# The fourth group's output in seven products, x added to the products of the last three groups, the last substitution spread into the fifth period, two scalings moved to VectorE

## The chip, the cores and the metric

The kernel runs on one core of a Trainium2 chip. The metric is the device time of one execution in microseconds; lower is better. All arithmetic is float32.

## The reference

Two blocks follow each other. The first is a delta-rule recurrence over 768 tokens for each of 4 batches and 8 heads of 48 dimensions; the second is a feed-forward layer with a maximum over three hidden projections, for 3072 tokens of width 384 and a hidden width of 768.

```python
k_n = k / (np.linalg.norm(k, axis=-1, keepdims=True) + 1e-06)
for t in range(S):
    kt, vt, bt = (k_n[:, :, t], v[:, :, t], beta[:, :, t, None])
    y[:, :, t] = np.einsum('bhd,bhde->bhe', q[:, :, t], state)
    v_old = np.einsum('bhde,bhd->bhe', state, kt)
    state = state + bt[:, :, :, None] * np.einsum('bhd,bhe->bhde', kt, vt - v_old)
...
x = attn_out.transpose(0, 2, 1, 3).reshape(B * S, H * D)
h = np.maximum(np.maximum(x @ w1, x @ w2), x @ w3)
out = h @ w_out
```

## The kernel before

**Chunks and groups.** The recurrence is solved in 12 chunks of 64 tokens. A chunk needs a triangular inverse, which VectorE finds by substitution: `solve(m)` does it for the two chunks of group `m` at once, in 31 steps of a pair of operations, a product into `tmp` (L563) and a subtraction (L567). The generator `solving` is stepped by `some(solving, n)`. When it ends, `solve` writes the result to DRAM (`y_d`, L588) and reads it back in another layout into `ut` (L597), both on SyncE's queue. The products `z` and `j` (`join_z`, `join_u`) complete the inverse; `new` (p_u) gives the chunk's new values, from the scaled values `v_t` less what the state already holds (`old_k`: p_k on TensorE, then L754 on VectorE); `step` (p_s) adds to the state `st` (L800); `to_y` (p_y, L814) gives the chunk's output y.

**From y to x.** `y_blocks` writes y to DRAM (`y_x`), `read_y` reads it back into `qall`, both on SyncE's queue, and `turn_y` (L872) transposes it on VectorE into `xt`, the x of the feed-forward layer.

**Periods.** Two chunks make a group of 512 tokens, and there are six groups, `m` = 0 to 5, here the first to the sixth. `ffn(m)` is a generator that runs the feed-forward layer of group `m`: one period. After each of its units it yields, and the loop at the end of the kernel puts in pieces of the recurrence of group `m + 1` by the tables `LINKS` and `LAST_LINKS`. In them, a letter is a piece and a digit its chunk or block: k, q, z, j, u, s and y are the products above; d the transposes `turn_t1`; x is `y_blocks`, w `read_y`, X `turn_y`; V loads values and P or p scales them; K loads keys; L and N load blocks; t and g turn them and form the key products. The entry 17 of `LINKS` puts X1 after unit 17. The order of instructions on each engine is the order in which the code issues them; nothing reorders it. So where VectorE waits, all that the code issued later for VectorE waits too.

**Hidden layer.** In the second to the fifth period a period has six hidden tiles of 128 columns for two differences of weights, 12 units, each of three matmuls 512 wide (p_h, L1170); ScalarE takes the first of a tile (L1180), VectorE the maximum (L1184). The sixth does it in products of quarters (`crossed_hidden`), whose weights `cross_hidden` makes in the fifth period (L1072). It makes sums of quarters of x as well (L1094 to L1097).

**Output.** For the first four groups `ffn` multiplies four token tiles with `wo_sb` (six matmuls 384 wide) and, from the second group on, adds x times `w_sb[0]` (three more), both L1209. For the fifth and sixth group `outputs` does it in seven products of halves (L971): the halves of h, three matrices each, are added and subtracted on VectorE (`op`, L1000) before the products, the results after them, and the two banks p and q are used in turn. The x part stands outside the seven products there, as plain products `x_times` of three slices for each quarter of the result. `cross_weights` makes the combinations of `wo_sb` that the seven products need, on VectorE, in the fifth period, after units 8 and 9 (L925 to L944).

**Banks.** `ps_ffn` has two PSUM banks until the sixth period, and p_h, p and q share them. A product into a bank starts when the last reader of the bank is done.

**Scaling.** `scale` (L298) multiplies the values of chunk `c` with their norms, on GpSimd for all chunks.

Of the kernel before, what the change touches and what calls it, by code (L numbers as in the profile page):

```python
# [9 lines left out]
FP32 = mybir.dt.float32  # L10
# [4 lines left out]
ALU = mybir.AluOpType  # L15

C = 64
# [6 lines left out]
def kernel(  # L24
# [31 lines left out]
    nc = tc.nc  # L56
# [5 lines left out]
    KT = DM // 128  # L62
    FT = DFF // 128
    NP = H // 2
    UNITS = NCH * 2
    GROUPS = UNITS // 4
# [22 lines left out]
    def ps_ffn(shape, name):  # L89

        one = len(pools) > 1
        return pools[-1].tile(shape, FP32, name=name, tag="ffn", bufs=8 if one else 2)
# [202 lines left out]
            nrms[2 * m + cc] = t[:, 16:32].rearrange("p (g h) -> p g h", g=2)  # L295

    def scale(c, nrm):
        nc.gpsimd.tensor_tensor(  # L298
            out=vts[c], in0=vts[c],
            in1=nrm[:, :, :, None].to_broadcast([128, 2, H, D]), op=ALU.mult,  # L300
        )
# [16 lines left out]
    def square(name):  # L318
        return work.tile([128, H, C], FP32, name=name, tag="square", bufs=17)
# [594 lines left out]
    HALF = DM // 2  # L914
# [3 lines left out]
    def cross_weights(part):  # L918

        left, right = slice(0, HALF), slice(HALF, DM)  # L920
        top, bottom = wo_sb[:, 0:PAIRS], wo_sb[:, PAIRS:FT]
        spare = w_sb[0][:, :, DM : 2 * DM]
        minus = nc.vector.tensor_tensor
        if part == 0:
            minus(  # L925
                out=spare[:, :, right], in0=bottom[:, :, right], in1=top[:, :, right],
                op=ALU.subtract,
            )
            minus(
                out=top[:, :, right], in0=top[:, :, right], in1=top[:, :, left],  # L930
                op=ALU.subtract,
            )
            return
        minus(
            out=spare[:, :, left], in0=bottom[:, :, right], in1=top[:, :, right],
            op=ALU.subtract,
        )
        fourth = []
        for n in range(2):
            t = work.tile([128, DM], FP32, name="mant", bufs=2)  # L940
            for i in range(2 - n):
                fourth.append(t[:, HALF * i : HALF * (i + 1)])
        for j in range(PAIRS):
            minus(  # L944
                out=fourth[j], in0=wo_sb[:, PAIRS + j, left], in1=spare[:, j, left],
                op=ALU.subtract,
            )
        crossed.update(
            b11=[top[:, j, left] for j in range(PAIRS)],
            b21=[bottom[:, j, left] for j in range(PAIRS)],  # L950
            b22=[bottom[:, j, right] for j in range(PAIRS)],
            t1=[top[:, j, right] for j in range(PAIRS)],
            t2=[spare[:, j, left] for j in range(PAIRS)],
            t3=[spare[:, j, right] for j in range(PAIRS)],
            t4=fourth,
        )

    def outputs(m, hs):


        xt, w = xts[m], crossed
        a11, a21, a12, a22 = (
            [hs[j + d][:, lo : lo + 256] for j in range(PAIRS)]
            for d, lo in ((0, 0), (0, 256), (PAIRS, 0), (PAIRS, 256))
        )
        p, q = (ps_ffn([128, 2, HALF], "p_o") for _ in range(2))

        def times(to, a, b, start=True, stop=True):
            for g in range(2):
                for j in range(PAIRS):  # L970
                    nc.tensor.matmul(  # L971
                        to[:, g], a[j][:, 128 * g : 128 * (g + 1)], b[j],
                        start=(start and g == j == 0),
                        stop=(stop and g == 1 and j == PAIRS - 1),
                    )

        def x_times(to, lo, right, start=False, stop=True):
            times(
                to,
                [xt[:, t, lo : lo + 256] for t in range(KT)],  # L980
                [w_sb[0][:, t, HALF * right : HALF * (right + 1)] for t in range(KT)],
                start, stop,
            )

        def held(name, dtype_bufs):
            return work.tile([128, 2, HALF], FP32, name=name, bufs=dtype_bufs)

        def store(o, cc, right, queues=one_queue):
            cols = slice(HALF * right, HALF * (right + 1))
            s0 = (2 * m + cc) * C  # L990
            for n in range(2):
                queues[n].dma_start(
                    out=out.rearrange("(b s) d -> b s d", s=S)[
                        2 * n : 2 * n + 2, s0 : s0 + C, cols
                    ].rearrange("g c x -> c g x"),
                    in_=o[rows(n)],
                )

        def op(to, a, b, how):
            nc.vector.tensor_tensor(out=to, in0=a, in1=b, op=how)  # L1000

        plus, minus = ALU.add, ALU.subtract
        times(p, a11, w["b11"])
        m1 = held("m1", 1)
        nc.scalar.copy(m1, p)
        yield
        sums = [square("s").rearrange("p h c -> p (h c)") for _ in range(PAIRS)]
        s14, s32 = ([s[:, lo : lo + 256] for s in sums] for lo in (0, 256))
        for j in range(PAIRS):
            op(s32[j], a11[j], a21[j], minus)  # L1010
        for j in range(PAIRS):
            op(s14[j], a21[j], a22[j], plus)
        times(q, a12, w["b21"], True, False)
        yield
        x_times(q, 0, 0)
        c11 = held("o_sb", 2)
        op(c11, m1, q, plus)
        store(c11, 0, 0)
        yield
        times(p, s32, w["t3"])  # L1020
        m7 = held("o_sb", 2)
        nc.scalar.copy(m7, p)
        yield
        times(q, s14, w["t1"])
        m5 = held("up", 2)
        nc.scalar.copy(m5, q)
        for j in range(PAIRS):
            op(s32[j], s14[j], a11[j], minus)
        yield
        times(p, s32, w["t2"])  # L1030
        m6 = held("up", 2)
        nc.scalar.copy(m6, p)
        for j in range(PAIRS):
            op(s14[j], a12[j], s32[j], minus)
        yield
        x_times(q, 0, 1, True, False)
        op(m6, m6, m1, plus)
        op(m7, m7, m6, plus)
        yield
        times(p, a22, w["t4"], True, False)  # L1040
        op(m6, m6, m5, plus)
        op(m5, m5, m7, plus)
        yield
        x_times(p, 256, 0)
        op(m7, m7, p, plus)
        store(m7, 1, 0)
        yield
        times(q, s14, w["b22"], False)
        op(m6, m6, q, plus)
        store(m6, 0, 1)  # L1050
        yield
        x_times(p, 256, 1, True)
        op(m5, m5, p, plus)
        store(m5, 1, 1, both_queues)
        yield

    thirds = {}

    def cross_hidden(i):

# [17 lines left out]
    def crossed_hidden(m, hs):  # L1078
# [16 lines left out]
        vec(out=s1, in0=a21, in1=a22, op=ALU.add)  # L1095
        vec(out=s2, in0=s1, in1=a11, op=ALU.subtract)
        vec(out=s4, in0=a12, in1=s2, op=ALU.subtract)  # L1097
        for j in range(FT):
            hs[j] = square("h").rearrange("p h c -> p (h c)")
        for unit in range(2 * PAIRS):  # L1100
# [58 lines left out]
    def ffn(m):  # L1159
# [35 lines left out]
            early = FT  # L1195
        for f in range(early, FT):
            yield from hidden(f, 0, TOK)
        if m >= GROUPS - 2:
            yield from outputs(m, hs)
            return  # L1200
        for i in range(4):
# [21 lines left out]
    def some(gen, n):  # L1223
        for _ in range(n):
            if next(gen, gen) is gen:
                break
# [102 lines left out]
        5: "g2 g3 p1", 6: "u0 N0", 7: "V1 N1", 8: "s0 y0 N2", 9: "x0", 10: "k1 q1",  # L1329
        11: "u1 w0", 13: "y1 x1 s1", 14: "X0 w1", 16: "P0", 17: "X1 K0 K1 K2 K3",  # L1330
    }
    LAST_LINKS = {**LINKS, 17: "", 19: "X1"}
    EARLY_LINKS = {
        9: "k0 q0", 10: "t0", 11: "t1", 12: "g0", 13: "t2", 14: "g1", 15: "t3",
        16: "g2", 17: "g3", 18: "d0 d1 z0 z1", 19: "j0", 20: "j1 u0", 21: "s0",
# [22 lines left out]
    def links(m, names):  # L1358
        for name in names.split():
            f, i = name[0], int(name[1])  # L1360
            if f in RECURS and m < GROUPS:
                RECURS[f](2 * m + i)
            elif f in MADE and m + 1 < GROUPS:
                MADE[f](2 * (m + 1) + i)
            elif f in UNIT and m + 1 < GROUPS:
                UNIT[f](4 * (m + 1) + i)
            elif f == "N" and m + 2 < GROUPS:
                load_blocks(4 * (m + 2) + i)
# [67 lines left out]
    MADE.update(V=lambda c: load_v(c, nc.gpsimd))  # L1436
    for m in range(1, GROUPS):
        for i, _ in enumerate(ffn(m)):
            if i == 0:
                some(solving, 3)  # L1440
            if m == 1 and i in (2, 5, 8):
                both_layers(i // 3)
            if m == GROUPS - 2 and i in (4, 5):
                cross_hidden(i - 3)
            if m == GROUPS - 2 and i in (8, 9):
                cross_weights(i - 8)
            if m + 2 < GROUPS:
                if i == 6:
                    blocks(m + 2)
                if i == 8:  # L1450
                    solving = solve(m + 2)
            links(m + 1, (LAST_LINKS if m == GROUPS - 2 else LINKS).get(i, ""))
            if i > 7:
                some(solving, 3 if i > 8 else 1)
    by_hand.close()
# [28 lines left out]
```

## Time and profile before

| | |
|---|---|
| Median of 3 runs | 511.67 us (509.7 to 511.67) |
| Profiled execution | 512.05 us, its span 510.2 us |
| TensorE busy | 489.5 us, 96% of the span |
| VectorE busy | 349.8 us, 69% |
| ScalarE, GpSimd busy | 168.8 us, 192.7 us |
| Fourth period | 316.4 to 389.2 us |
| Fifth period | 389.2 to 455.7 us |
| Sixth period | 455.7 to 510.2 us |
| TensorE, output of the fourth group | 363.9 to 389.2 us |
| TensorE, output of the fifth and the sixth | 432.1 to 455.1 us, 484.3 to 505.9 us |

Times are from one execution taken by the hardware profiler. PE is TensorE, DVE VectorE, ACT ScalarE, POOL GpSimd, SP SyncE; SPq is SyncE's queue, which issues DMAs. A row of an order in time gives the start, the duration, the engine, the line, the operation, what it writes and reads, and how often; in brackets stands how long the engine was idle before it and what ended that. A float32 matmul has two records.

### The profile page before, as it was taken

How to read it: one execution, taken by the hardware profiler on the slowest of the kernel's cores; microseconds unless marked ns; L12 is line 12 of the kernel's file. 1: busy time of each engine (PE TensorE's matmuls, PEld its weight loads, DVE VectorE, ACT ScalarE, POOL GpSimd, SP SyncE). 2: the span in 40 equal slices, each digit the busy share in tenths (PEclk: the TensorE clock that was granted, in tenths of full speed). 3: DMA queues.
4: the chain of work that ended last, by engine and by line, in shares of the span. 5: the costliest groups of instructions: out<-in, count | busy, mean ns of one | idle time of the engine just before them, and what ended most of it. 6: DMA issues, size and time to landing. Idle time of an engine off the chain costs nothing.

```text
span 510.2 us, 18525 instructions
## 1 busy us (share of the span) xinstructions
PE 489.5 (96%) x8016; PEld 333.6 (65%) x8016; DVE 349.8 (69%) x801; ACT 168.8 (33%) x320; POOL 192.7 (38%) x317
## 2 busy tenths in 40 slices
PE   7678989999999999999999999999999999999996
PEld 6567768855566555565555565555565556988896
DVE  5887789977997341799562988554988446458752
ACT  5585655785422142210153200252101321112310
POOL 7434462793491935780485690601230000000000
PEclk9855889999999999999999999999999999999999
DMA  8937869674045934454585354834334302230001
GB/s 111 202 53 213 189 148 168 172 182 144 3 125 132 192 64 99 123 124 109 120 156 128 106 136 96 167 52 90 91 80 97 67 1 62 50 78 2 0 17 46
DMA packets 106304, 53.49 MB, mean 105 GB/s; under 512 B 89712, under 2 KB 99984, under 8 KB 106224
## 3 DMA queue, kind: packets, MB, share of 16 engines
q1 hardware_dynamic: 94352, 31.35, 30.2%
q0 software_dynamic: 9472, 20.37, 16.0%
q8 instruction: 63, 1.03, 0.9%
q10 hardware_dynamic: 2400, 0.59, 0.6%
q14 instruction: 17, 0.14, 0.1%
HBM read 39.17 MB, written 13.11 MB: 102 GB/s over the span
## 4 chain that ended last, share of the span: by engine, by line
PE 77%; DVE 7%; DMA 6%; ACT 4%; SPq 3%; issue 2%; POOL 0%; DVEq 0%; ACTq 0%; POOLq 0%
PE p_h L1170 28%; PE p_o L1209 17%; PE p_o L971 8%; PE p_e L1113 3%; PE p_c L1113 3%; PE p_u L770 2%; PE p_g L417 2%; PE p_m L905 2%; DMA qall<-in_q_dram 2%; PE p_s L793 2%; DMA kmore<-in_k_dram 2%; PE p_y L812 2%; SPq L131 2%; PE p_k L742 2%; PE p_j L725 2%
## 5 line engine op out<-in xcount | busy, mean ns | idle before, releaser
L1170 PE MATMUL p_h<-xt,w_sb 128*128 128x512 f32 (+1 forms) x450 | 188.9, 562 | 0.7 <-ACT xt L838 0.6
L1170 PEld LDWEIGHTS p_h<-xt,w_sb 128*128 128x128 f32 x450 | 83.2, 195 | 69.0 <-issue 61.8
L1209 PE MATMUL p_o<-wo_sb,h 128*128 128x384 f32 x192 | 65.3, 490 | 0.0
L1184 DVE TENSOR_TENSOR h<-h,p_h 128x512 f32<-128x512 f32 (+1 forms) x42 | 25.5, 607 | 54.1 <-PE p_h L1170 53.4
L563 DVE TENSOR_TENSOR tmp<-x_bl,y_bl 128x31 f32<-128x31 f32 (+20 forms) x139 | 51.2, 368 | 4.1
L567 DVE TENSOR_TENSOR y_bl<-y_bl,tmp 128x31 f32<-128x31 f32 (+20 forms) x139 | 48.5, 349 | 4.8
L1209 PEld LDWEIGHTS p_o<-wo_sb,h 128*128 128x128 f32 x192 | 35.7, 190 | 23.2
L375 POOL DMA_DIRECT2D turned<-in_q_dram x72 | 39.3, 553 | 5.4 <-POOL turned L370 3.1
L1215 ACT COPY o_sb<-p_o 128x384 f32<-128x384 f32 x16 | 7.7, 479 | 85.8 <-PE p_o L1209 79.7
L1180 ACT ACTIVATE h<-p_h 128x512 f32<-128x512 f32 x24 | 14.3, 597 | 62.9 <-PE p_h L1170 59.9
L265 POOL TENSOR_TENSOR w_sb<-mant,up 128x384 int32<-128x384 int32 x18 | 18.8, 1044 | 41.2 <-DVE mant L261 39.1
L417 PEld LDWEIGHTS p_g<-kqt 48*64 48x64 f32 x1216 | 24.1, 138 | 9.3 <-issue 6.2
L417 PE MATMUL p_g<-kqt 48*64 48x64 f32 (+1 forms) x1216 | 27.4, 238 | 1.0 <-ACT kqt L346 0.8
L800 DVE TENSOR_TENSOR st<-st,p_s 48x768 f32<-48x768 f32 (+1 forms) x18 | 17.1, 949 | 15.4 <-PE p_s L793 15.2
L131 POOL DMA_DIRECT2D kpad<-in_k_dram x32 | 21.9, 692 | 14.0 <-issue 12.6
L1209 PE MATMUL p_o<-w_sb,xt 128*128 128x384 f32 x72 | 25.2, 486 | 0.0
L401 DVE TENSOR_TENSOR pt<-p_g,mask 128x512 f32<-128x512 f32 x20 | 13.8, 689 | 16.1 <-PE p_g L417 15.8
L150 POOL DMA_DIRECT2D v_t<-in_v_dram x14 | 11.6, 831 | 34.7 <-PE p_u L770 34.7
L298 POOL TENSOR_TENSOR v_t<-v_t,nrm 128x768 f32<-128x768 f32 x12 | 17.9, 1495 | 9.0 <-DVE nrm L292 8.9
L370 POOL MEMSET turned<- 128x96 f32 x18 | 3.3, 192 | 46.9 <-DVE kqt L391 46.9
L770 PEld LDWEIGHTS p_u<-v_t,ut 64*64 64x64 f32 x768 | 13.5, 141 | 9.8 <-issue 8.6
L1209 PEld LDWEIGHTS p_o<-w_sb,xt 128*128 128x128 f32 x72 | 13.7, 190 | 9.5
(212 smaller groups left out, 835.4 us busy)
## 6 DMA issues: line engine op xcount, KB each, us to landing
out_dram<-o_sb SPq DMA_DIRECT2D x40, 96.0 KB
w_bits<-in_moe_w_dram SPq DMA_DIRECT2D x9, 384.0 KB
w_bits<-in_moe_w_dram POOLq DMA_DIRECT2D x9, 384.0 KB, 5.1
turned<-in_q_dram POOLq DMA_DIRECT2D x72, 48.0 KB, 2.9
kpad<-in_k_dram POOLq DMA_DIRECT2D x32, 96.0 KB, 5.5
y_x<-y SPq DMA_DIRECT2D x16, 192.0 KB
qall<-y_x SPq DMA_DIRECT2D x32, 96.0 KB
v_t<-in_v_dram POOLq DMA_DIRECT2D x14, 192.0 KB, 4.8
```

The costliest lines, as they stand in the source:

```text
L131: queues[bb].dma_start(out=dst[rows(bb ^ g), :, 0:D], in_=src[2 * bb + g, :, c * C : (c + 1) * C, :].rearrange("h p d -> p h d"),)
L265: nc.gpsimd.tensor_tensor(out=dst.bitcast(I32), in0=mant_v.bitcast(I32), in1=up_v, op=ALU.add)
L375: (queue, nc.gpsimd)[i].dma_start(out=t[p0 : p0 + 32, bb, at : at + NP * 2 * D].rearrange("p (j x) -> p j x", j=NP), in_=(k, q)[i][2 * bb ...
L417: nc.tensor.matmul(p_g[rows(bb ^ (g * i)), par, c0 : c0 + C * (1 + whole)], kq[:, 0], kq if whole else kq[:, i],)
L563: nc.vector.tensor_tensor(out=t_v, in0=row.to_broadcast(t_v.shape), in1=column.to_broadcast(t_v.shape), op=ALU.mult,)
L567: nc.vector.tensor_tensor(out=rest, in0=rest, in1=t_v, op=ALU.subtract)
L770: nc.tensor.matmul(p_v[rows(bb ^ g), g, i], ut[c % NU][rows(bb), g, h], rhs[rows(bb), g, h],)
L971: nc.tensor.matmul(to[:, g], a[j][:, 128 * g : 128 * (g + 1)], b[j], start=(start and g == j == 0), stop=(stop and g == 1 and j == PAIRS - 1),
L1113: nc.tensor.matmul(to, w[stays], moves, start=(n == 0), stop=(n == len(terms) - 1))
L1170: nc.tensor.matmul(p_h, w_sb[i][:, t, f * 128 : (f + 1) * 128], xt[:, t, lo : lo + w], start=(t == 0), stop=(t == KT - 1),)
L1184: nc.vector.tensor_tensor(out=h, in0=h, in1=p_h, op=ALU.max)
L1209: nc.tensor.matmul(p_o, stays, moves, start=(n == 0), stop=(n == len(terms) - 1))
```

## The change

The fourth group's output is done by `outputs` too. In `outputs`, two of the three slices of x join the halves of h: each of the four quarters gets one more matrix, so a product has 8 matmuls instead of 6, and `x_times` keeps one slice, 2 matmuls instead of 6. A group's output has 7 x 8 + 4 x 2 = 64 matmuls of 192 columns; before, the fifth and sixth had 7 x 6 + 4 x 6 = 66, and the fourth 36 of 384. `cross_weights` gets a third part, four subtractions on 128x192, for the weights of x; its three parts now run in the fourth period after units 5, 6 and 10. The sums of x are made with those of h in the fourth and fifth period, in four matrices instead of three; the sixth uses those that `crossed_hidden` makes anyway. In the fourth period the sums lie in `kmore`.

The fourth and fifth period get tables of their own. In the fourth (now of 23 units) the turns X0 and X1 go from units 14 and 17 to 15 and 18, the scaling P0 from 16 to 21. The substitution of the last group was ended within the fourth period and the first three steps of the fifth; now 20 steps are taken in the fourth and 17 in units 0 to 5 of the fifth. The products that need its result go later there: z from unit 3 to 7, j to 8, the first u from 6 to 9, s and y from 8 to 10, k and q of the second chunk from 10 to 11, the second u to 12. `scale` runs on VectorE for chunks 10 and 11.

```diff
     def scale(c, nrm):
-        nc.gpsimd.tensor_tensor(
+        (nc.vector if c > 9 else nc.gpsimd).tensor_tensor(
...
+        if part == 2:
+            x11, x12, x21, x22 = (w_sb[0][:, t, lr] for t in range(2) for lr in (left, right))
+            free = work.tile([128, NP, 2, 2, C], FP32, name="kqt", bufs=6)
...
+            for to, a, b in ((x3, x22, x12), (x1, x12, x11), (x2, x22, x1), (x4, x21, x2)):
+                minus(out=to, in0=a, in1=b, op=ALU.subtract)
+            for name, x in dict(
+                b11=x11, b21=x21, b22=x22, t1=x1, t2=x2, t3=x3, t4=x4
+            ).items():
+                crossed[name].append(x)
+            return
...
+        for a, t, lo in ((a11, 0, 0), (a21, 0, 256), (a12, 1, 0), (a22, 1, 256)):
+            a.append(xt[:, t, lo : lo + 256])
...
         def x_times(to, lo, right, start=False, stop=True):
             times(
                 to,
-                [xt[:, t, lo : lo + 256] for t in range(KT)],
-                [w_sb[0][:, t, HALF * right : HALF * (right + 1)] for t in range(KT)],
+                [xt[:, KT - 1, lo : lo + 256]],
+                [w_sb[0][:, KT - 1, HALF * right : HALF * (right + 1)]],
                 start, stop,
             )
...
-        sums = [square("s").rearrange("p h c -> p (h c)") for _ in range(PAIRS)]
+        n = len(x_sums.get(m, ())) == 0
+        if m == GROUPS - 3:
+            sums = [
+                t.rearrange("p a h d -> p (a h d)")[:, lo : lo + 512]
+                for t in kmore
+                for lo in (0, 512)
+            ]
+        else:
+            sums = [
+                square("s").rearrange("p h c -> p (h c)") for _ in range(PAIRS + n)
+            ]
         s14, s32 = ([s[:, lo : lo + 256] for s in sums] for lo in (0, 256))
-        for j in range(PAIRS):
-            op(s32[j], a11[j], a21[j], minus)
-        for j in range(PAIRS):
-            op(s14[j], a21[j], a22[j], plus)
+        s1, s2, s3, s4 = s14, s32, s32, s14
+        if not n:
+            s1, s2, s3, s4 = (s + [x] for s, x in zip((s1, s2, s3, s4), x_sums[m]))
+        for j in range(len(sums)):
+            op(s3[j], a11[j], a21[j], minus)
+        for j in range(len(sums)):
+            op(s1[j], a21[j], a22[j], plus)
...
-        if m >= GROUPS - 2:
+        if m >= GROUPS - 3:
             yield from outputs(m, hs)
...
-    LAST_LINKS = {**LINKS, 17: "", 19: "X1"}
+    FOURTH_LINKS = {
+        **LINKS, 14: "w1", 15: "X0", 16: "", 17: "K0 K1 K2 K3", 18: "X1", 21: "P0",
+    }
+    LAST_LINKS = {
+        0: "k0 q0", 6: "p1", 7: "d0 d1 z0 z1", 8: "j0 j1", 9: "u0", 10: "s0 y0",
+        11: "x0 k1 q1", 12: "u1 w0", 13: "y1 x1", 14: "w1", 15: "X0", 19: "X1",
+    }
+
+    STEPS = {
+        GROUPS - 3: {8: 1, **dict.fromkeys((9, 10, 11), 3), 12: 2, 14: 1, 15: 1, 18: 1, 19: 1, 20: 2, 21: 1, 22: 1},
+        GROUPS - 2: {0: 2, 1: 3, 2: 3, 3: 3, 4: 3, 5: 3},
+    }
...
-            if i == 0:
+            if i == 0 and m < GROUPS - 2:
                 some(solving, 3)
...
-            if m == GROUPS - 2 and i in (8, 9):
-                cross_weights(i - 8)
+            if m == GROUPS - 3 and i in (5, 6, 10):
+                cross_weights((5, 6, 10).index(i))
...
-            links(m + 1, (LAST_LINKS if m == GROUPS - 2 else LINKS).get(i, ""))
-            if i > 7:
+            late = {GROUPS - 3: FOURTH_LINKS, GROUPS - 2: LAST_LINKS}
+            links(m + 1, late.get(m, LINKS).get(i, ""))
+            if m in STEPS:
+                some(solving, STEPS[m].get(i, 0))
+            elif i > 7:
                 some(solving, 3 if i > 8 else 1)
```

## The prediction

> **What bounds the kernel now.** I read the page's busy times first, then the table by stretches for the periods that the change touches, then the list of waits of TensorE, then the order in time of each engine from 314 us on.
>
> ```profile
> span 510.2 us, 18525 instructions
> ...
> PE 489.5 (96%) x8016; PEld 333.6 (65%) x8016; DVE 349.8 (69%) x801; ACT 168.8 (33%) x320; POOL 192.7 (38%) x317
> ```
>
> TensorE sets the time. The stretches below are the second part of the fourth period (351.4 to 389.2) and the whole fifth (389.2 to 455.7).
>
> ```profile
> core 0: us, PE busy (x) PEld busy (x) DVE busy (x) ACT busy (x) POOL busy (x), PEclk, DMA share, GB/s
> ...
> 351.40:389.20 37.80, 37.70 (x497) 22.61 (x487) 33.89 (x73) 4.95 (x10) 8.36 (x10) 1.00 0.33 83
> 389.20:455.70 66.50, 65.89 (x1037) 45.78 (x1036) 33.93 (x69) 13.83 (x23) 0.00 (x0) 1.00 0.23 52
> ```
>
> TensorE has no gap in the first and 0.6 us in the second, but VectorE, with 33.89 of 37.80 us, has little time to give in the first; that is where the change puts its additions. From 316 us on TensorE's list of waits has one line:
>
> ```profile
> PE p_c L1113 <- DVE up L1000: 0.6, 1, 0.6
> ```
>
> What the products cost, in TensorE's order in time (a tile of nine 384 wide, then the next period's first; then two products of six, 192 wide):
>
> ```profile
> 383.40 4.03 PE L1209 MATMUL p_o<-wo_sb,h 128*128 128x384 f32 x12
> 387.27 2.10 PE L1209 MATMUL p_o<-w_sb,xt 128*128 128x384 f32 x6
> 389.20 2.77 PE L1170 MATMUL p_h<-xt,w_sb 128*128 128x512 f32 x6
> ...
> 441.27 2.11 PE L971 MATMUL p_o<-wo_sb,s 128*128 128x192 f32 x12
> 443.23 2.11 PE L971 MATMUL p_o<-w_sb,s 128*128 128x192 f32 x12
> ```
>
> A matmul has two records. Start to start, 384 columns cost 5.80/9 = 0.645 us and 192 cost 1.96/6, over longer runs 0.325.
>
> VectorE and SyncE's queue around the second output of a period (y, its round trip through DRAM, its turn L872 into xt):
>
> ```profile
> 361.30 0.95 DVE L754 TENSOR_TENSOR v_t<-v_t,p_k 128x768 f32<-128x768 f32 x1
> ...
> 371.16 0.95 DVE L814 TENSOR_TENSOR y<-qs,p_y 128x768 f32<-128x768 f32 x1 [1.62 <-PE p_y L812]
> ...
> 374.87 2.81 DVE L563 TENSOR_TENSOR tmp<-x_bl,y_bl 128x252 f32<-128x252 f32 x1
> ...
> 387.80 1.22 DVE L872 STREAM_TRANSPOSE xt<-qall 128x768 f32<-128x768 f32 x1
> ...
> 450.78 1.23 DVE L872 STREAM_TRANSPOSE xt<-qall 128x768 f32<-128x768 f32 x1 [2.50 <-DMA qall<-y_x]
> 451.92 0.52 DVE L1000 TENSOR_TENSOR o_sb<-o_sb,p_o 128x384 f32<-128x384 f32 x1
> ```
> ```profile
> 372.64 1.16 SPq L850 DMA_DIRECT2D y_x<-y  x2
> 381.43 2.54 SPq L861 DMA_DIRECT2D qall<-y_x  x4
> ...
> 393.21 1.09 SPq L588 DMA_DIRECT2D y_d<-y_bl  x2
> 396.68 4.04 SPq L597 DMA_DIRECT2D ut<-y_d  x8
> ```
>
> The turn at 387.80 ended 0.2 us before the fifth period's first matmul needed it. The turn at 450.78 stood 2.50 us in VectorE's queue waiting for its DMA, and an add that frees a bank stood behind it; TensorE needed that bank at 452.98, half a microsecond later.
>
> **The products.** The fourth group loses 36 matmuls of 384 and gets 64 of 192: 36 x 0.645 = 23.2 against 64 x 0.325 = 20.8, so -2.4 us. The fifth and sixth groups go from 66 to 64: -0.65 each. All of it lies on the path as long as TensorE never waits: -3.7 in all.
>
> The Trainium skill's page "TensorE: Matmul & The Clock Gate", section "Back-to-back issue gap", speaks against halving the width: it gives a sustained spacing of 81 ns at 128 columns and 131 at 512, so narrow matmuls do not get proportionally cheaper. A straight line between them, my estimate, makes 192 columns 0.78 of 384, and by that the fourth group would lose about 9 us instead of gaining 2.4. The rows above have half the width at half the time, and I go by them.
>
> **VectorE's list in the fourth period, up to the second turn.** Two steps of cross_weights now come before the maskings at 340.66. The first (0.75 + 0.76 from L925 and L929) delays them by 1.1 us, and with them the copies, the stores at_d and the load x_bl; the substitution's first operation began at 354.57 with 0.9 us of cover, so 0.2 is left. Against that, the scaling on GpSimd (356.37 to 357.85) no longer holds VectorE: L535 took 0.72 there where a neighbour of its size takes 0.19, so -0.5. The four new subtractions, 128x192, are priced by L944 (three in 0.90), with their hand-overs 1.4 us; they stand ahead of L754, for which p_u on TensorE waits. Before, L754 ended 362.25 and p_u began 362.81, some 0.45 of cover: TensorE waits 1.4 + 0.2 - 0.5 - 0.45 = 0.6 there.
>
> From there I lay VectorE's list end to end, at the spacings of before. L754 ends 363.0; three pairs of the substitution (L563, L567) 1.9; the max 0.6; five pairs 4.1: 369.5. Eight sums of 128x256 (L1000 has six in 2.10, so 0.34 each) 2.7: 372.2. Now y, 0.9: **373.15, 1.04 later than before**, although p_y has been done since 371. The state (two, 1.75) and the first output's add (0.5) follow: 375.4. TensorE's fourth product needs the bank that this add frees, and is ready at 375.0: wait 0.5. A pair, the first turn, a pair (2.9): the next four sums begin at 378.3, where product t2 is ready at 378.1: wait 0.6. Then the sums, and two adds at 382.1: VectorE gets to the second turn at 383.3, not behind the bank-freeing adds as in the fifth period of before but **ahead** of them.
>
> **The second turn.** Its data: y ended 372.11, SyncE issued y_x at 372.64 (0.5 late, behind a store), qall at 381.43, its last issue ended 383.97, and landing takes 1.9 to 2.2 more (448.91 to 450.78 in the fifth period, 311.49 to 313.72 in the third). That is 13.9 us, 13.4 without the late issue. So the turn starts at 373.15 + 13.4 = 386.6, and VectorE idles 3.3 us. Behind it, in its queue: a pair, two adds, a pair, the add that frees p (0.55), two pairs, the add that frees q. Pairs are 0.85 to 0.9 and adds 0.55: with the turn's 1.2 the first bank is free at 391.0, the second at 386.6 + 1.2 + 5.5 = 393.3. TensorE, at its last product at 388.0, waits 3.0 for the first, and 1.6 for the second, in which the fifth period's first p_h goes. So the fifth period starts at 393.3 instead of 389.2: **+4.1**, with the 2.4 of saved products and the small waits already in it. The round trip has two bounds in the trace: 12.4 (438.41 to 450.78, few other transfers) and 14.4 (299.33 to 313.72, beside all key loads). I take 13.4 since the same K2 and K3 loads run beside it; the ends give +3.1 and +5.1. The scaling of c=10 on VectorE (no such row there; GpSimd took 1.49, y on VectorE 0.95) comes behind all that and, with P0 moved to unit 21, delays no one that waits.
>
> **The fifth period.** The substitution now ends there. VectorE is lined up with TensorE by L754, which waits for p_k (period start + 3.55, so 396.85). After it: L754 0.9, two pairs, a wait for the first max, two maxima, the four crossings of L1072 (2.2), and in all twelve pairs, whose like took 383.71 to 393.18 with a turn of 1.1 in it, 8.3. With 1.1 us of wait that is 13.9: the substitution ends at 410.9. Then y_d and ut: before, it ended 393.18 and the second z product followed at 402.5 without a gap, after a last ut issue that ended at 400.72 and needs its landing of about 2; so between 7.5 and 9.3, I take 9.1: 420.0. TensorE, with z moved from unit 3 to 7, is ready for that product at 393.3 + 2.6 + 2.0 + 7 x 2.6 + 0.65 = 416.7. **+3.4** (1.7 at the lower bound). Before, 8.7 us of other products lay between the substitution's end and the first z; now 5.1 (410.9 to 416.0) do. The second crossing and the scaling of c=11 stand behind y_d on VectorE and hold nothing up: u0 has moved to unit 9. The round trip of the last y has less room too: 12.4 plus turn and add make 15.2 against 46 products of 0.325 plus a restart, 15.1: +0.1.
>
> **Sum.** +4.1 (fourth) - 0.65 + 3.4 + 0.1 (fifth) - 0.65 + 0.1 (sixth, 0.1 for a hand-over from sums to product) = +6.4. The profiled execution took 512.05 (span 510.2 and 1.85 around it), 0.4 above the median of the three runs, 511.67. 512.05 + 6.4 = **518.4**.
>
> **Rivals.** (a) TensorE stays the clock; that is the faster side. Place: the bank of the last product in the fourth period. The second turn would have to start by 382, a round trip of 9 us, and ut to land 5.8 us after the substitution: 508.3. TensorE's gapless record speaks for it; no round trip in the trace is so short. With short trips alone VectorE's list still starts the fifth period at 390.0 and the sum is -0.3, no change. (b) Only the ut wait vanishes, because VectorE overtakes in the fifth period: 515.0. L754's wait for p_k speaks against it. (c) The trip takes 14.4 and the x_bl load slips by another 1: 520.4. (d) The change does not do what it says: narrow matmuls cost more than half, or more copies than expected; the rows of 192 in the fifth and sixth periods speak against it.
>
> **Numbers.** The forecast 0.7, with its own range 515.7 (12.4 trip, ut at 7.5) to 519.6; (a) 0.12, half of it at no change; (b) 0.1; (c) 0.06; (d) 0.02. Leaving out (a) and part of the outer tails: 514.0 to 520.5. About 0.5%, 2.6 us, is what a measurement of this kernel can tell from no change. Faster 0.06, same 0.06, slower 0.88.
>
> **What would show it.** Right: a wait of TensorE of about 3 us for an add on VectorE at the end of the fourth period, with VectorE idle for qall just before; 1.6 at the next period's first p_h; 3 us ahead of p_z for ut in the fifth. The step on the round trip is wrong if the second turn starts before 385, that on the substitution if p_z has no wait. If 192-wide records come at more than 0.17 us each, the products were mispriced. No wait of TensorE over 1 us in either period would make the forecast wrong altogether.

## The result, and the profile after

The changed kernel took 522.65 us (median of 6 runs, 521.5 to 526.15) where the kernel before took 511.67 (6 runs, 509.7 to 512.3): a ratio of 1.0234, with a 95% interval from 1.0205 to 1.0262. The prediction was 518.4, with a range up to 520.5: the sign is right, the size is short by 4.25 us. Between the medians the change is 11.0 us, and the forecast's sum was 6.4, so the sum is 4.6 short; the forecast set out from the profiled execution of before, 512.05, which is 0.4 above the median. The profiled execution took 523.21 us, 11.2 more than that of before. The ratios here and below leave out disturbed executions, so they need not be the quotient of the medians.

The page of the changed kernel: the span, TensorE's busy time, and the clock that TensorE was granted, in 40 slices of the span.

```profile
span 521.1 us, 18655 instructions
...
PE 492.1 (94%) x8064; PEld 340.6 (65%) x8064; DVE 359.1 (69%) x835; ACT 168.7 (32%) x320; POOL 189.6 (36%) x315
...
PEclk9855899999999999999999999999998979999999
```

TensorE does 48 more records and is busy 2.6 us longer, but the span grew by 10.9. And the clock row has an 8 and a 7 late in the span, where the row of before has nines:

```profile
PEclk9855889999999999999999999999999999999999
```

Line numbers have moved in the changed kernel: L971 (the products of the output) is now L985, L1000 (its sums and adds) L1014, L1113 (p_c) L1141 and L1170 (p_h) L1198. TensorE's waits from 300 us on, total, how often, longest:

```profile
PE p_z L712 <- DMA ut<-y_d: 3.1, 3, 1.8
PE p_o L985 <- DVE o_sb L1014: 2.4, 2, 2.1
PE p_h L1198 <- DVE up L1014: 1.3, 1, 1.3
PE p_u L770 <- PE p_h L1198: 0.8, 1, 0.8
PE p_c L1141 <- DVE up L1014: 0.6, 1, 0.6
PE p_o L985 <- DVE kmore L1014: 0.2, 1, 0.2
```

Before, only the 0.6 at p_c was there. The waits that are new sum to 7.8 us; the products give some 3 back. The order in time of the changed kernel (VectorE, SyncE's queue, TensorE) shows how the two large ones arise:

```profile
372.06 0.94 DVE L814 TENSOR_TENSOR y<-qs,p_y 128x768 f32<-128x768 f32 x1
...
385.91 1.24 DVE L872 STREAM_TRANSPOSE xt<-qall 128x768 f32<-128x768 f32 x1 [2.77 <-DMA qall<-y_x]
...
389.67 0.54 DVE L1014 TENSOR_TENSOR o_sb<-o_sb,p_o 128x384 f32<-128x384 f32 x1
...
391.85 0.55 DVE L1014 TENSOR_TENSOR up<-up,p_o 128x384 f32<-128x384 f32 x1
...
411.56 0.21 DVE L567 TENSOR_TENSOR y_bl<-y_bl,tmp 128x31 f32<-128x31 f32 x1
```
```profile
373.03 1.14 SPq L850 DMA_DIRECT2D y_x<-y  x2
...
381.35 2.54 SPq L861 DMA_DIRECT2D qall<-y_x  x4
...
411.84 1.12 SPq L588 DMA_DIRECT2D y_d<-y_bl  x2
415.28 4.77 SPq L597 DMA_DIRECT2D ut<-y_d  x8
```
```profile
390.27 0.92 PE L985 MATMUL p_o<-w_sb,xt 128*128 128x192 f32 x4 [2.14 <-DVE o_sb L1014]
392.45 4.54 PE L1198 MATMUL p_h<-xt,w_sb 128*128 128x512 f32 x6 [1.26 <-DVE up L1014]
...
419.03 0.25 PE L712 MATMUL p_z<-ut,at 32*32 32x32 f32 x4 [1.80 <-DMA ut<-y_d]
419.57 0.72 PE L712 MATMUL p_z<-ut,at 32*32 32x32 f32 x60 [0.30 <-DMA ut<-y_d]
421.29 1.46 PE L712 MATMUL p_z<-ut,at 32*32 32x32 f32 x64 [1.00 <-DMA ut<-y_d]
422.68 5.04 PE L1198 MATMUL p_h<-xt,w_sb 128*128 128x512 f32 x6
```

VectorE stood 2.77 us for qall, and the adds that free TensorE's banks (389.67 and 391.85) stood behind it: TensorE waits 2.14 before its last product and 1.26 before the fifth period's first p_h, which starts at 392.45 (before: 389.20). The substitution ended at 411.8, and its result was on its way when TensorE reached p_z at 417.2. All of these steps had been forecast.

What had not been forecast is in the second column: p_h took 4.54 and 5.04 us where six such records took 2.77 before (at 389.20), and the second half of p_z took 1.46 where 64 such records otherwise take 0.7. The table by stretches has the reason; the column ahead of the DMA share is the granted clock:

```profile
392.40:397.00 4.60, 4.55 (x10) 1.69 (x14) 2.82 (x6) 0.00 (x0) 0.00 (x0) 0.63 0.41 99
397.00:398.90 1.90, 1.90 (x128) 1.87 (x128) 0.77 (x1) 0.60 (x1) 0.00 (x0) 1.00 0.05 9
...
421.30:422.70 1.40, 1.32 (x65) 1.13 (x65) 0.58 (x2) 0.21 (x1) 0.00 (x0) 0.50 0.00 0
422.70:427.70 5.00, 5.00 (x12) 1.87 (x14) 0.00 (x0) 1.15 (x2) 0.00 (x0) 0.56 0.01 3
```

In both places TensorE ran at half its clock: for 3.4 us from 393.0, right behind the two waits for VectorE, and for 6.8 us from 420.3, after the first two of the three waits for ut. By the starts, the first p_h lost 1.76 us (4.47 against 2.71), the second z product 0.7, the p_h behind it 2.2: 4.7 us in all, which is the size of the miss. With the waits of 7.8 and the products' 3.0 that makes 9.5 of the span's 10.9; the rest, some tenths in each of the three periods and in the tail behind TensorE's last product, was not followed up.

### The profile page after: what moved, and what is told of

Read it like the earlier page. It is cut to its first block, busy times and chain, and to the rows that moved or that the text cites. A ratio compares the mean times of both kernels' runs of the same rounds, so it can differ in the third digit from the quotient of the medians.

```text
span 521.1 us, 18655 instructions
## 1 busy us (share of the span) xinstructions
PE 492.1 (94%) x8064; PEld 340.6 (65%) x8064; DVE 359.1 (69%) x835; ACT 168.7 (32%) x320; POOL 189.6 (36%) x315
## 4 chain that ended last, share of the span: by engine, by line
PE 71%; DVE 11%; DMA 8%; ACT 4%; SPq 3%; issue 2%; POOL 1%; DVEq 0%; ACTq 0%; POOLq 0%
PE p_h L1198 26%; PE p_o L1237 12%; PE p_o L985 9%; PE p_e L1141 3%; DMA qall<-in_q_dram 3%; PE p_g L417 3%; PE p_c L1141 3%; PE p_m L905 2%; PE p_u L770 2%; DVE tmp L563 2%; PE p_k L742 2%; DMA kmore<-in_k_dram 2%; PE p_y L812 2%; PE p_s L793 1%; DMA y_x<-y 1%
## 5 line engine op out<-in xcount | busy, mean ns | idle before, releaser
L1198 PE MATMUL p_h<-xt,w_sb 128*128 128x512 f32 (+1 forms) x450 | 191.5, 569 | 1.8 <-DVE up L1014 1.3
L1198 PEld LDWEIGHTS p_h<-xt,w_sb 128*128 128x128 f32 x450 | 83.7, 196 | 72.1 <-issue 63.1
L563 DVE TENSOR_TENSOR tmp<-x_bl,y_bl 128x31 f32<-128x31 f32 (+20 forms) x139 | 48.9, 352 | 3.8
L1237 PE MATMUL p_o<-wo_sb,h 128*128 128x384 f32 x144 | 48.9, 490 | 0.0
L1237 PEld LDWEIGHTS p_o<-wo_sb,h 128*128 128x128 f32 x144 | 26.7, 190 | 17.2
L1243 ACT COPY o_sb<-p_o 128x384 f32<-128x384 f32 x12 | 5.8, 480 | 62.6 <-PE p_o L1237 56.5
L434 ACT COPY at<-p_g 128x512 f32<-128x512 f32 x22 | 12.8, 586 | 18.7 <-DVE pt L401 16.3
L716 ACT COPY z<-p_z 32x512 f32<-32x512 f32 (+1 forms) x26 | 14.1, 543 | 13.4 <-PE p_z L712 13.0
L754 DVE TENSOR_TENSOR v_t<-v_t,p_k 128x768 f32<-128x768 f32 x11 | 10.4, 950 | 11.2 <-PE p_k L742 11.2
```

Source lines behind the costliest of these rows:

```text
L563: nc.vector.tensor_tensor(out=t_v, in0=row.to_broadcast(t_v.shape), in1=column.to_broadcast(t_v.shape), op=ALU.mult,)
L1198: nc.tensor.matmul(p_h, w_sb[i][:, t, f * 128 : (f + 1) * 128], xt[:, t, lo : lo + w], start=(t == 0), stop=(t == KT - 1),)
L1237: nc.tensor.matmul(p_o, stays, moves, start=(n == 0), stop=(n == len(terms) - 1))
```

## The experiments

**Theory A** was: the loss is TensorE's waits, put there by VectorE's order and by the late substitution, plus a halved clock that the waits bring about. **Theory B**: the clock drops on its own or by load, and the waits only happen to lie beside it. **Theory C**: the narrow products or the added operations themselves cost the time.

The totals of one kernel spread over 1.2 to 7.4 us, and part of the spread arises before the change can act: the fourth period, before which all these kernels are alike, starts between 314.7 and 317.9 us in their traces. The half clock in the first 71 us differs too, 23.9 to 34.1 us in all, but it doesn't order these starts by itself (30.7 us of it stand beside 314.7 and beside 317.7), so what moves them is not shown. So the table has beside the totals the time in the profiled execution from the fourth period's first matmul to the end of TensorE's last one. The last column is the half clock after that start, up to TensorE's end. It is one execution for each kernel; the second and third period, alike in all of them, took 156.8 to 157.8 us together, so a difference of less than 1 us in these times says little.

| kernel | median us (runs) | ratio to before, 95% | from the fourth period's start | half clock there, us |
|---|---|---|---|---|
| before | 511.67 (6) | 1 | 189.5 | none |
| after | 522.65 (6) | 1.0234 [1.0205, 1.0262] | 200.3 | 3.4 + 6.8 |
| e1 second turn later | 518.82 (4) | 1.0150 [1.0097, 1.0204] | 195.9 | 6.8 |
| e2 substitution earlier | 517.69 (4) | 1.0129 [1.0076, 1.0182] | 194.2 | 3.4 |
| e3 waits filled | 518.18 (4) | 1.0136 [1.0079, 1.0193] | 194.9 | none |
| e4 y and substitution earlier | 513.48 (10) | 1.0047 [1.0011, 1.0082] | 190.2 | none |
| e5 tuned | 511.75 (12) | 0.9965 [0.9934, 0.9995] | 188.2 | none |
| e6 fourth group as before | 511.06 (12) | 0.9969 [0.9948, 0.9990] | 188.6 | none |
| e7 scaling on GpSimd | 522.42 (4) | 1.0195 [1.0140, 1.0249] | 200.0 | 3.4 + 3.4 |
| e8 half of the waits filled | 519.63 (10) | 1.0143 [1.0115, 1.0171] | 195.0 | none |

The kernel before, run beside them, had medians of 511.27 (e1 to e4, 13 runs) and 512.34 (e5 to e8, 29 runs).

**e1: only the second turn of the fourth period is moved.**

```diff
-        17: "K0 K1 K2 K3", 18: "X1", 21: "P0",
+        17: "K0 K1 K2 K3", 21: "X1 P0",
```

> Only the second turn of the fourth period (X1) is moved, from unit 18 behind both adds that free the banks, to unit 21. Theory A (the loss is TensorE's waits plus the halved clock that follows a wait): the 2.1 us before the last product of the fourth period vanish, a wait of about 1.3 us before the fifth period's first p_h stays, now for the turn; the fifth period starts 2.5 us earlier, and if the 2.1 us were what dropped the clock, the slow stretch at 393 to 396.4 us goes too, another 1.8 us. Time 518.3 (clock stretch gone) to 520.2 (stays) against 522.65. The 6.8 us stretch at 420 stays. Theory B (the clock drops on its own, or by load): both slow stretches stay where they are in the program, 520.2. Theory C (the narrow products or the added subtractions cost the time): no change, 522.6.

518.82 us; from the fourth period's start 4.4 us less than after. TensorE's order in time:

```profile
389.72 2.81 PE L1198 MATMUL p_h<-xt,w_sb 128*128 128x512 f32 x6 [1.20 <-DVE xt L872]
...
416.14 1.49 PE L712 MATMUL p_z<-ut,at 32*32 32x32 f32 x64 [1.09 <-DMA ut<-y_d]
417.57 5.49 PE L1198 MATMUL p_h<-xt,w_sb 128*128 128x512 f32 x6
```

The wait before the last product is gone, the 1.20 is there for the turn, and p_h ran at full clock: the first stretch is gone, though no matmul changed. The second stretch stayed, behind waits of 1.0, 0.3 and 1.1. Against B, the drop follows the wait; against C, an order in VectorE's list was worth 4 us.

**e2: only the substitution ends earlier.**

```diff
-            if m == GROUPS - 2 and i in (4, 5):
-                cross_hidden(i - 3)
+            if m == GROUPS - 2 and i in (9, 10):
+                cross_hidden(i - 8)
...
-        GROUPS - 3: {... 21: 1, 22: 1},
-        GROUPS - 2: {0: 2, 1: 3, 2: 3, 3: 3, 4: 3, 5: 3},
+        GROUPS - 3: {... 21: 1, 22: 4},
+        GROUPS - 2: {0: 2, 1: 3, 2: 3, 3: 3, 4: 3},
```

> Only the last substitution's end is moved: the two crossings of the fifth period go from units 4 and 5 (ahead of the substitution's last pairs) to units 9 and 10, and its last three pairs from unit 5 of the fifth period to the end of the fourth, where VectorE otherwise idles for p_k. By the trace's 2.1 us of crossings and 2.8 us of idle time, the substitution should end some 4.5 us earlier, near 407.2, and ut land near 414.5, before TensorE's 417.2. Theory A: all of the 3.1 us of waits before p_z vanish and with them the slow stretch at 420 to 427 us (0.7 in p_z, 2.2 in p_h): 516.6 against 522.65. The stretch at 393 stays. Theory B (the clock drops on its own): 519.5, with a slow stretch of 7 us still there. Theory C (narrow products or added subtractions): no change, 522.6.

517.69 us, 1.1 above what A had (516.6) and 1.8 below B's 519.5; from the fourth period's start it is 6.0 less than after, the 6.05 that A had. SyncE issued y_d 15.5 us after the fifth period's start instead of 19.4. TensorE:

```profile
393.84 4.36 PE L1198 MATMUL p_h<-xt,w_sb 128*128 128x512 f32 x6 [1.26 <-DVE up L1014]
...
419.60 0.72 PE L712 MATMUL p_z<-ut,at 32*32 32x32 f32 x60 [0.17 <-DMA ut<-y_d]
420.25 2.84 PE L1198 MATMUL p_h<-xt,w_sb 128*128 128x512 f32 x6
```

p_z began at 418.37 with no wait ahead of it. The mirror image of e1: the wait at the fourth period's end is untouched, and p_h behind it is still slow; the wait at p_z is nearly gone, and so is the slow p_h behind that.

**e3: nothing is moved, the waits are filled with matmuls that nobody reads.** Calls of `fill` stand around the last product (6 and 3 matmuls) and ahead of the two halves of p_z (5 and 2).

```diff
...
+    def fill(n):
+        p_w = ps_two("p_w").rearrange("p b x -> p (b x)")[:, 0:192]
+        for _ in range(n):
+            nc.tensor.matmul(p_w, ident, w_sb[0][:, 2, 0:192])
...
```

> Nothing is moved. Matmuls of 192 columns whose result nobody reads fill TensorE's waits: 6 and 3 around the last product of the fourth period, 5 before the first and 2 before the second half of p_z, at 0.325 us each, so that the work behind them starts no later than now. Theory A with the clock as a consequence of the waits: both slow stretches vanish, the fifth period's first p_h takes 2.8 us instead of 4.5, the second z product 0.7 instead of 1.5, the p_h behind it 2.8 instead of 5.0; in all 4.7 us, 518.0 against 522.65. Theory B (the clock drops by load or on its own): the stretches stay, 522.6 or more. If a single stretch vanishes: 520.9 (the first) or 519.7 (the second).

518.18 us. TensorE's order (p_h is L1202 here) and the clock row:

```profile
389.81 2.11 PE L1277 MATMUL p_w<-w_sb,ident 128*128 128x192 f32 x12
392.07 0.92 PE L985 MATMUL p_o<-w_sb,xt 128*128 128x192 f32 x4
392.82 1.14 PE L1277 MATMUL p_w<-w_sb,ident 128*128 128x192 f32 x6
394.24 2.84 PE L1202 MATMUL p_h<-xt,w_sb 128*128 128x512 f32 x6 [0.28 <-DVE up L1014]
...
421.29 2.84 PE L1202 MATMUL p_h<-xt,w_sb 128*128 128x512 f32 x6
```
```profile
PEclk9855899999999999999999999999999999999999
```

The fifth period starts as late as in after (76.3 us behind the fourth period's start in both), so the wait for VectorE is as long as it was; but the clock stays, and both p_h take 2.84. This settles it for A: none of the kernel's own work was moved or removed, TensorE only kept turning, and 4.5 us came back (5.3 from the fourth period's start; the substitution also ended 1.7 us earlier behind the fifth period's start, 17.6 against 19.3, since p_k follows the faster p_h and L754 waits for p_k).

**e8: only two of the four waits are filled**, the one before the last product (6 matmuls) and the one between the halves of p_z (2).

> As the third kernel, but only two of the four waits are filled with unread matmuls: the 2.1 us before the last product of the fourth period (the 1.3 behind it stay), and the 1.0 in the middle of p_z (the 1.8 and 0.3 ahead of it stay). Theory A says nothing of how much wait drops the clock; in the first kernel a single 1.2 did not, 2.4 in three pieces did. If it takes more than 2 us of wait within some 4 us: the first stretch vanishes, and the second shrinks or vanishes, 518.0 to 520.9. If any wait of over 1 us does it: both stay, 522.6. If the clock drops on its own: both stay where they are in the program.

519.63 us, and no half clock in the fourth to sixth period. TensorE:

```profile
392.99 2.84 PE L1200 MATMUL p_h<-xt,w_sb 128*128 128x512 f32 x6 [1.25 <-DVE up L1014]
...
416.75 0.25 PE L712 MATMUL p_z<-ut,at 32*32 32x32 f32 x4 [0.68 <-DMA ut<-y_d]
417.35 0.72 PE L712 MATMUL p_z<-ut,at 32*32 32x32 f32 x60 [0.35 <-DMA ut<-y_d]
```

The wait of 1.25 that was left did not drop the clock. That p_z would still wait 1.8 was wrong: with a fast first p_h the substitution ends earlier too, and 0.7, 0.35 and 0.4 were left. So one saved stretch of half clock paid twice here.

**e7: the scaling goes back to GpSimd.**

```diff
-        (nc.vector if c > 9 else nc.gpsimd).tensor_tensor(
+        nc.gpsimd.tensor_tensor(
```

> Only the scaling of the last two chunks' values goes back from VectorE to GpSimd. Theory A: VectorE's two scalings (0.95 us each) stand behind the add that the fifth period's first p_h waits for, and behind y_d, so no one waits for them; the same waits and the same two slow stretches, 522.6 within 0.6. Rival (the scaling on VectorE is part of the loss): 0.95 to 1.9 us less, 520.8 to 521.7.

522.42 us, no change in the total, but not with the same waits: product t2 waited 3.5 us for the sums, and the 2.1 before the last product was gone. The half clock moved with the wait: 3.4 us of it began at 381.24, behind the wait of t2, and p_h at the fifth period's start took 2.84. So the total agrees with what was expected, but not for the reason given. TensorE's wait, and its cause in VectorE's and GpSimd's order:

```profile
381.17 2.19 PE L985 MATMUL p_o<-w_sb,kmore 128*128 128x192 f32 x6 [3.49 <-DVE kmore L1014]
```
```profile
374.67 3.71 DVE L563 TENSOR_TENSOR tmp<-x_bl,y_bl 128x240 f32<-128x240 f32 x1
```
```profile
375.19 2.91 POOL L298 TENSOR_TENSOR v_t<-v_t,nrm 128x768 f32<-128x768 f32 x2
```

VectorE's product took 3.71 us; in after, where GpSimd does not do these scalings, the same one took 0.40:

```profile
375.34 0.40 DVE L563 TENSOR_TENSOR tmp<-x_bl,y_bl 128x240 f32<-128x240 f32 x1
```

In e7 it ended 0.3 us after GpSimd's two scalings did. The trace of before has the same: the row of 2.81 us at 374.87, quoted in the prediction and not read there, ended 0.3 us after this scaling:

```profile
375.90 1.49 POOL L298 TENSOR_TENSOR v_t<-v_t,nrm 128x768 f32<-128x768 f32 x1
```

So moving the scalings removes a stall of VectorE of 2.4 us (3.3 in e7), at the price of two scalings of 0.95 us on VectorE itself; no total here shows a gain from it. In e7 that stall delays the sums and hides the wait for qall; in after the stall is gone and VectorE idles for qall instead. The Trainium skill's page "GPSIMD Engine Reference", section "8. Key points", says that GpSimd shares its SBUF interfaces with VectorE and contends with it in operations with two SBUF inputs; the 3.71 against 0.40 agrees. It doesn't tell all: VectorE's product began 0.5 us (e7) and 1.0 us (before) ahead of the scaling's start on record, and what held it until then is not shown.

**e4: y a unit earlier, and the substitution as in e2.**

```diff
-        **LINKS, 14: "w1", ...
+        **LINKS, 12: "y1 x1 s1", 13: "", 14: "w1", ...
```

> The edit of the substitution as in the second kernel, and y, its state and its second x product are issued one unit earlier in the fourth period (unit 12, ahead of the eight sums on VectorE): y should end near 369.6 instead of 373.0, and its round trip of 12.9 us with the turn end near 383.7, behind which no add waits any more. Theory A: no wait over 1.4 us of TensorE in the fourth and fifth period and no slow stretch after 55 us. Against 522.65: 3.1 us of p_z waits, about 3 of the 3.7 at the end of the fourth period, 4.7 of slow clock: 511.9, level with the 511.67 of before. Theory B: the slow stretches stay, 516.6. Theory C (narrow products or added subtractions): 522.6.

513.48 us, 10.0 less from the fourth period's start, and no half clock. y ended at 368.1 instead of 373.0, the turn followed at 382.51 without waiting, and p_z did not wait. What was left were waits of at most 0.9 us, 3.3 in all. The 513.48 is 1.6 us above the 511.9 that was expected; the ratio is 1.0047 [1.0011, 1.0082]. Against e2, from which it differs by y alone, it is 4.0 less from the fourth period's start.

**e5: what stands ahead of those waits on VectorE goes behind them.** On top of e4:

```diff
-                cross_weights((5, 6, 10).index(i))
+                cross_weights((5, 6, 11).index(i))
...
-        0: "k0 q0", 6: "p1", 7: "d0 d1 z0 z1", 8: "j0 j1", 9: "u0", 10: "s0 y0",
-        11: "x0 k1 q1", 12: "u1 w0", 13: "y1 x1",
+        0: "k0 q0", 6: "p1", 8: "d0 d1 z0 z1", 9: "j0 j1", 10: "u0", 11: "s0 y0 k1 q1",
+        12: "x0 u1 w0", 13: "y1 x1",
...
+        GROUPS - 3: {8: 1, 9: 3, 10: 3, 11: 3, 12: 0, 14: 1, 15: 1, 18: 1, 19: 1, 20: 0, 22: 4},
+        GROUPS - 2: {0: 3, 1: 3, 2: 3, 3: 3, 4: 5},
```

> The fourth kernel's edits, and four more that take VectorE's work out from in front of the remaining waits: the four subtractions of the weights go from unit 10 to 11 (behind the addition that p_u waits for), the substitution's pairs of units 12 and 20 of the fourth period go to unit 22 and the fifth period, and z, j and u0 of the fifth period are issued one unit later. Theory A (each wait of TensorE was VectorE's order): the 0.8 at p_u, the 1.1 at the sums and most of the 0.8 at the fifth period's first p_h vanish, 1.0 appears where s0 and k1 now share a unit. From the fourth period's start to TensorE's last product before needs 189.5 us and the fourth kernel 190.2; expected here 188.0, and about 509.8 us where before has 511.3. Rival (VectorE has no room left, what is freed in one place is late in the next): 190 or more, 511.5 to 513.

All of TensorE's waits from 300 us on:

```profile
PE p_k L742 <- DVE st L800: 0.7, 1, 0.7
PE p_c L1141 <- DVE up L1014: 0.6, 1, 0.6
```

188.2 us from the fourth period's start, where 188.0 was expected, and a ratio of 0.9965 [0.9934, 0.9995]: the change, with VectorE's list put in order, is ahead of after by 2.6% (from the two ratios) and of before by 0.35%, little more than the interval.

**e6: the fourth group's output as before, the fifth and sixth as changed.**

```diff
-        if m >= GROUPS - 3:
+        if m >= GROUPS - 2:
             yield from outputs(m, hs)
...
-            if m == GROUPS - 3 and i in (5, 6, 10):
-                cross_weights((5, 6, 10).index(i))
+            if m == GROUPS - 2 and i in (8, 9, 10):
+                cross_weights((8, 9, 10).index(i))
...
```

The fourth period has the table and the steps of before again, so the substitution ends where it did before; the fifth keeps the later table of the change.

> The fourth group's output goes back to its nine products of whole width, with the order and the substitution of before; the fifth and sixth groups keep x in their seven products, and the crossed weights are made in the fifth period again (units 8, 9, 10). Theory A: no wait over 0.7 us of TensorE after 314 us, no slow stretch, and the two groups give 0.65 us each: from the fourth period's start to TensorE's last product 188.2 us against 189.5 of before, and 510.0 us where before has 511.3. Rival (x in all three products costs more in sums and in waits than it saves): 189.5 or more, 511.3 and above.

A ratio of 0.9969 [0.9948, 0.9990] and 188.6 us from the fourth period's start, 1.0 less than before, where 1.3 was expected. So two matmuls fewer in each of the last two groups are worth about what they promise, and the loss in after came with the fourth group's output and the order of VectorE's work that was changed for it, the later substitution included. Between e5 and e6 these runs do not decide.

## Why the prediction was right on the sign and wrong on the size

- **Products.** Right in kind, a little large in the fourth group. 192-wide records came at 0.163 us each in all three groups, so (d) is out. In e5, where TensorE has no wait there, the fourth group's output takes 23.5 us (362.24 to 385.75, the next p_h) against 25.3 before (363.88 to 389.20): -1.8, not -2.4. The first records after a change of operands are longer (six in 1.24 instead of 1.14), and there are more such changes.
- **The wait at p_u, t1, t2.** Forecast 0.6, 0.5, 0.6; measured 0.8, 0.3, 0.2. GpSimd's scaling no longer stretched L535 (0.19), as forecast.
- **The second turn.** The mechanism was right, step by step: VectorE idle 2.8 (forecast 3.3) ahead of the turn at 385.91 (386.6), TensorE's waits 2.1 and 1.3 (3.0 and 1.6), the fifth period's start 3.25 later (4.1). The round trip took 12.9, not 13.4.
- **The substitution in the fifth period.** The mechanism was right. It ended at 411.8 (forecast 410.9), since the slow p_h brought p_k, and so L754, 1.3 us later; p_z waited 3.1 in all (3.4).
- **The step that failed is the sum.** It took both waits at their own length and let everything behind them run at the spacings of before. The fourth period grew by 3.5 us (forecast 4.1) and the sixth shrank by 0.5 (forecast 0.55), but the fifth grew by 7.7 where the sum has 3.4 + 0.1 - 0.65 = 2.85. The term that is missing there is the clock, which the sum put at nothing: 1.8 us behind the first wait, 0.7 + 2.2 behind the second, 4.7 together. e3 shows it by itself, e1 and e2 one stretch each. The rows of before gave a granted clock of 1.00 in both periods, but they show a TensorE without waits there; they are no evidence of what it does after one. The early slices of the same page, where the clock row shows 5, were not asked what had gone before them.
- **Rivals.** (a) and (b) fell with the waits; (c) did not come, the trip was shorter; (d) has the rows against it. None of them had the clock in it, which is why the range ended at 520.5.

## What to carry to other kernels

A wait of TensorE can cost more than its length: where two or more microseconds of waits come close together, add what a half clock behind them takes (here 1.8 and 2.9 us), and remember that several short waits add up. Where such a wait can't be removed, matmuls that nobody reads can keep the clock up. When work is added to an engine with little room, write out its list to the end of the stage, and look what its late items hold: here one transpose ahead of two adds was worth 4 us, and moving it (e1), or making its data earlier (e4 against e2), was all that it took.

## What the runs showed of the hardware

- **How much waiting drops the clock.** Full clock stayed after a single wait of 1.2 us (e1), after 0.3 + 1.25 (e8) and after 0.7 + 0.35 + 0.4 at p_z (e8). It fell to half after 2.1 + 1.3 and after 1.8 + 0.3 (after; the 1.0 that followed found it down already), 2.2 + 0.9 (e2, within its second wait), 1.0 + 0.3 + 1.1 (e1), and 3.5 and 1.8 + 0.3 + 0.9 (e7). So in these runs 1.55 us of waits within some 4 us left the clock alone, 2.1 us could bring it down, and no single wait needs to be long. The drop does not come at once: in e7 the clock stayed full for 2.9 us behind the 1.8 + 0.3. And the clock changes of one run lie multiples of 3.41 us apart (the drops at 393.00 and 420.31 in after are eight of them apart). Cut into such steps, TensorE was idle for 1.9 and 2.1 us (after), 2.4 (e1), 2.5 (e2), 3.3 and 1.4 (e7) of the step that ended with a drop, and for at most 1.8 us (e7) of any other between the fourth period's start and the end of TensorE's work. So some 1.9 us of idle time within one step fits five of the six drops; no run was made to test it. The half clock lasted 3.4 or 6.8 us each time. The Trainium skill's page "TensorE: Matmul & The Clock Gate", section "HAM oscillation — how this bites in real kernels", gives the rule that gaps should stay under some 3.4 us; here 2.4 us in three pieces, the longest 1.1 (e1), were enough, so the measurement is the stricter. Its section "What's actually happening" has a free-running window of 3413 ns, and the stretches of 3.4 and 6.8 us are one and two of those.
- **A two-input operation of VectorE that meets one of GpSimd** took 2.81 (before) and 3.71 us (e7) instead of 0.4, and ended 0.3 us after GpSimd was done.
- **The start differs from execution to execution.** The start of the fourth period lies up to 3.2 us apart for the same code ahead of it. Stages are better compared from a mark behind that than by totals.
